# Loads of gate i and x per chunk of 1024 tokens in a gated linear recurrence with a causal gated unit

## The chip, the cores and the metric

The kernel runs on one core of a Trainium2 chip. The metric is the device time of one execution in microseconds (us), taken as the median of several runs. The core has a matrix engine (PE, whose weight loads are listed as PEld), a vector engine (DVE), an activation engine (ACT), a general engine (POOL), a queue that issues transfers (SP) and 16 DMA engines that all transfers share.

## What is computed

The inputs have 4 sequences of 6336 tokens with 256 channels, in fp32. A linear recurrence over time runs first, and its result `y` goes through a gated unit with a causal convolution of five taps:

```python
log_a = 8.0 * sigmoid(r_gate) * np.log(np.clip(sigmoid(a_param), 1e-06, 1.0 - 1e-06))
a_t = np.exp(log_a)
norm = np.sqrt(np.maximum(1.0 - a_t * a_t, 1e-06))
x_gated = norm * sigmoid(i_gate) * x
for t in range(S):
    h = a_t[:, t] * h + x_gated[:, t]
    y[:, t] = h
# then, with x = y:
for k in range(5):
    gate_pre += conv_w[k] * xp[:, k:k + S, :]      # xp is x with four zero tokens ahead
out = (1.0 / (1.0 + np.exp(-gate_pre)) * (x @ w_val)) @ w_out
```

Three inputs (r, i, x) are read and one output is written, 25.95 MB each.

## The kernel before

**Tiling.** The 25344 tokens of all sequences are laid end to end and cut into 28 chunks: 256, 256 and 512 tokens, 23 chunks of 1024, and again 512 and 256. A chunk of 1024 is two windows of 512; there are 51 windows. Recurrence, roots and norm go by chunk, and the gated unit and its output go by window.

**Layouts.** A load puts tokens on the partitions: partition p holds consecutive tokens of its stretch, each with 256 channels. The recurrence needs channels on the partitions and time along the row, so work goes back and forth through transposes on PE, which write to PSUM (8 banks of 2 KB a partition).

**Rings.** `rring`, `iring` and `xring` have four slots each, a slot being one window (512 tokens, 4 KB a partition). The r load already takes a whole chunk in one transfer of 1 MB: partition p gets eight consecutive tokens, 8 KB, spread over two neighbouring slots (`of_chunk`, L281). The loads of i and x go window by window (`load`, L276): 512 KB, four consecutive tokens or 4 KB for each partition.

**Steps of a chunk or window**, by their names in the order:

- `lr`, `li`, `lx`: loads by SP. `ta` (L297) and `tb` (L300): tanh of r and i on ACT, for a whole chunk.
- `tr` (L345): PE transposes the tanh of r; `ex` (L359): ACT makes the decay `a` of it, in fp32, in the order of time, into `aring`.
- `sq` (L367): POOL squares the decay into `ering`; `rt` (L392): ACT takes the square root for a batch of up to four chunks and writes the norm as bf16. This needs another table of functions on ACT, so a table load (L543) stands before and after.
- `nt` (L406): PE transposes the norm back to tokens on partitions. The bf16 norm is taken as words of 4 B, each holding two neighbouring tokens of one channel, so a window of 512 tokens has 256 words and one transpose takes 128 of them: word q of every partition, that is every second word of the window's row.
- `pp`, `up` (L307, L319): POOL adds 1 to the tanh of i and multiplies by x, into `uring`. For six windows at the start and later (0 to 3, 8, 10) PE (`xp`, L324) copies x to PSUM and DVE (`uv`, L333) does the work.
- `xg` (L417): DVE multiplies the norm, out of PSUM, into `uring`, for a chunk. The last three chunks go another way (L421), without `nt`.
- `xt` (`words`, L431): PE transposes the words of `uring` to time along the row, each transpose writing every second word of its window in PSUM. `sc` (L464): DVE runs the recurrence as a scan over the chunk, once for each half of the channels.
- `cv` (L476): PE does the convolution, `tg` (L483): ACT the gate's tanh; `vl` (L491): PE the value product; `gv` (L496): DVE gate times value; `ou` (L506): PE the output product; `cd` or `ca` (L514, L516): DVE or ACT copies it out of PSUM; `st` (L527): SP stores it.

**Order.** `ORDER` is a list written out by hand or program beforehand; it is walked once, and each word emits the instructions of one step (the number after `@` are PSUM banks). Every engine runs its own instructions in that order, waiting where a buffer or an input isn't ready. SP's queue holds loads and stores together in the order, so one that waits for a slot holds up those behind it. The table of ACT functions is switched where the list asks for another.

Of the kernel before, what the change touches and what calls it, by code (L numbers as in the profile page):

```python
# [8 lines left out]
P = 128  # L9
CONV_K = 5  # L10
FP32 = mybir.dt.float32
# [13 lines left out]
NU = 10  # L25
NRI = 4
# [15 lines left out]
s_ident s_small s_kt s_diag lr.0 lr.2 lr.1 li.0 li.1 ta.0 ta.2 lr.3 tr.0.0@1 ex.0.0 ta.1 tr.2.0@1 tb.0 tr.2.1@4 lr.5  # L42
tr.1.0@2 li.2 ex.2.1 tr.1.1@6 tr.0.1@7 lx.2 ex.0.1 lx.0 ex.1.1 sq.0.1 ex.1.0 sq.1.1 ex.2.0 sq.2.1 ta.3 sq.0.0 sq.1.0
tb.1 lr.7 ta.4 li.4 li.3 lx.3 s_wl.3 tb.2 tr.3.0@6,7 s_wl.0 lx.1 ex.3.0 lr.9 tr.3.1@4,5 xp.0@2 ex.3.1 sq.3.0 li.6 uv.0
ta.5 s_wl.2 sq.2.0 sq.3.1 xp.2@2,3 lx.4 uv.2 tb.3 li.5 sq.4.1 s_wl.1 xp.3@6,7 uv.3 xp.1@1 sq.4.0 rt.0.0 lx.5 uv.1 li.7
li.8 pp.4 rt.1.0 nt.0@7 nt.2@6 xg.0 lx.6 nt.1@1 xt.0.1@4 xt.0.0@7 xg.1 xg.2 xt.1.1@2 sc.0.0 xt.2.1@5 up.4 xt.1.0@1
sc.1.0 sc.0.1 nt.3@6,7 sc.1.1 s_wcast lx.8 ta.6 lr.11 sc.2.1 cv.0@2,3 xt.2.0@4 cv.1@0,1 sc.2.0 tb.4 lr.13 xg.3 vl.1@4,5
tg.1 li.10 pp.5 tg.0 xt.3.1@6 gv.1 lx.7 tb.5 xt.3.0@7 pp.6 sc.3.1 tr.5.0@2,3 up.6 ex.5.0 tr.5.1@4,5 li.11 li.12
vl.0@0,1 gv.0 pp.7 sc.3.0 lx.10 ex.5.1 li.9 nt.4@0,1 up.5 ou.0.0@3 ou.1.0@2 ta.7 cd.0.0 cv.3@4,5 cd.1.0 st.0 sq.6.0
xg.4 lx.9 cv.2@6,7 tg.3 lr.15 tg.2 sq.5.1 st.1 vl.2@0,1 xt.4.0@3 ta.8 gv.2 cv.4@4,5 sq.5.0 sc.4.0 tg.4 lr.17 tr.7.0@6,7  # L50
xt.4.1@1 ex.7.0 sq.6.1 tr.7.1@4,5 sc.4.1 ex.7.1 xp.8@2,3 up.7 lx.12 uv.8 ou.2.0@6,7 cv.5@0,1 tb.6 sq.7.1 cd.2.0
vl.5@4,5 tb.7 li.13 sq.8.0 vl.4@2,3 lx.11 li.14 gv.4 tg.5 xp.10@6,7 li.16 sq.8.1 uv.10 st.2 li.15 ou.4.0@2,3 lx.14 gv.5
sq.7.0 rt.2.0 vl.3@6,7 gv.3 ou.5.0@0,1 pp.9 cd.4.0 pp.11 cd.5.0 rt.2.1 ou.3.0@2,3 up.9 cd.3.0 st.5 nt.5@6,7 xg.5
nt.6@0,1 up.11 lx.13 cv.6@2,3 st.3 xg.6 xt.5.0@5 xt.5.1@0 pp.12 lx.15 sc.5.0 tg.6 up.12 tb.8 xt.6.1@2 sc.5.1 nt.7@4,5
ta.10 pp.14 up.14 xg.7 ta.9 cv.8@6,7 lr.21 sc.6.1 xt.7.1@5 pp.13 tg.8 lr.19 vl.6@0,1 lx.16 tb.9 up.13 li.17 gv.6
tr.9.0@6,7 li.18 lx.18 sc.7.1 ex.9.0 li.19 pp.15 tr.9.1@0,1 lx.17 xt.6.0@4 li.20 pp.16 cv.7@2,3 ex.9.1 sc.6.0 sq.9.0
xt.7.0@5 st.4 ou.6.0@6,7 tg.7 up.15 vl.8@0,1 sc.7.0 ta.12 cv.9@2,3 sq.9.1 tg.9 cd.6.0 vl.7@4,5 ta.11 gv.7 nt.8@2,3
sq.10.0 xg.8 vl.9@6,7 tb.10 lr.23 st.6 tr.11.0@4,5 up.16 gv.9 lr.25 tr.11.1@2,3 ex.11.0 gv.8 ou.9.0@6,7 pp.18 cd.9.0
ou.7.0@0,1 ex.11.1 pp.17 xt.8.0@5 cd.7.0 sq.11.0 ou.8.0@6,7 st.7 xt.8.1@0 cd.8.0 tb.11 li.22 cv.11@2,3 lx.19 sq.10.1
sc.8.1 st.8 cv.10@6,7 tg.11 lx.20 li.21 ta.13 cv.12@2,3 li.23 sq.12.0 sc.8.0 tg.12 vl.12@0,1 lr.27 up.17 tg.10 li.24  # L60
vl.11@2,3 gv.11 vl.10@4,5 sq.11.1 rt.3.0 gv.10 sq.12.1 gv.12 ou.10.0@4,5 cd.10.0 ou.11.0@2,3 up.18 rt.3.1 cd.11.0
ou.12.0@4,5 cd.12.0 pp.19 lx.22 nt.9@0,1 st.10 xg.9 pp.20 lx.21 nt.10@6,7 st.11 up.19 xg.10 st.9 xt.9.1@5 xt.9.0@2
sc.9.1 cv.13@6,7 ta.14 up.20 tg.13 sc.9.0 lr.29 nt.11@4,5 tb.12 cv.14@6,7 xg.11 tg.14 li.26 pp.22 tr.13.1@2,3 st.12
xt.10.1@0 tb.13 li.25 up.22 sc.10.1 vl.14@4,5 lx.23 cv.15@6,7 ex.13.1 li.28 lx.24 pp.21 gv.14 vl.13@0,1 pp.24 tg.15
gv.13 vl.15@4,5 sq.14.1 ta.15 xt.10.0@7 gv.15 tr.13.0@0,1 sc.10.0 cv.16@2,3 sq.13.1 ex.13.0 lr.31 li.27 ou.13.0@4,5
up.21 ta.16 cd.13.0 ou.14.0@6,7 ou.15.0@0,1 cd.14.0 tg.16 lr.33 sq.13.0 nt.12@4,5 lx.25 cd.15.0 tb.14 xt.11.0@7 st.13
lx.26 xg.12 tr.15.0@2,3 pp.23 st.14 ex.15.0 tr.15.1@0,1 sc.11.0 up.23 cv.18@4,5 tg.18 xt.11.1@2 pp.25 sc.11.1 ex.15.1
vl.18@6,7 cv.17@4,5 up.24 tg.17 gv.18 vl.17@2,3 sq.14.0 lx.28 tb.15 li.29 gv.17 vl.16@0,1 st.15 xt.12.1@5 gv.16 pp.26
ta.17 li.31 ou.17.0@6,7 lx.27 cv.20@2,3 sc.12.1 sq.15.1 li.30 ta.18 cv.19@0,1 sq.16.0 cd.17.0 tg.20 ou.16.0@4,5 cd.16.0
tg.19 sq.15.0 vl.19@6,7 xt.12.0@2 gv.19 st.16 lr.37 vl.20@0,1 sq.16.1 lr.35 sc.12.0 rt.4.0 li.32 ou.18.0@6,7  # L70
ou.19.0@4,5 up.26 gv.20 cd.19.0 rt.4.1 up.25 nt.13@2,3 cd.18.0 nt.14@0,1 xg.13 pp.27 lx.29 cv.21@4,5 lx.30 xg.14 pp.28
st.19 xt.13.1@7 st.17 sc.13.1 up.27 st.18 tr.17.0@2,3 tg.21 ou.20.0@0,1 tb.16 up.28 lx.31 cd.20.0 vl.21@6,7 xt.13.0@4
ex.17.0 gv.21 li.34 tr.17.1@0,1 li.33 pp.29 sc.13.0 lx.32 nt.15@6,7 pp.30 ex.17.1 ou.21.0@2,3 sq.17.0 xt.14.0@5 xg.15
xt.14.1@4 ta.19 cv.22@0,1 sc.14.1 up.29 tg.22 lr.39 vl.22@6,7 tb.17 cv.23@0,1 sq.17.1 gv.22 sc.14.0 cv.24@6,7 tg.23
li.35 pp.32 lx.33 tg.24 li.36 pp.31 vl.23@0,1 ca.21.0 gv.23 up.30 ou.22.0@6,7 ta.20 xt.15.0@5 cd.22.0 cv.26@0,1 up.31
# [31 lines left out]
def kernel(  # L107
# [74 lines left out]
    with tc.manual_schedule():  # L182
# [101 lines left out]
        def op_li(w):  # L284
            load(w, "i")

        def op_lx(w):
            load(w, "x")
# [286 lines left out]
```

## Time and profile before

| what | value |
|---|---|
| median of three runs | 285.41 us (285.11 to 285.95) |
| the profiled execution's own time | 286.67 us |
| its span, from the first to the last instruction | 284.9 us |
| granted TensorE clock, mean | 1.000 |
| HBM read / written | 78.39 MB / 25.95 MB |
| packets of DMA queue q1 | 26640 |

The profile lists for each engine its busy time; for groups of instructions (by line, engine, operation and shape) the count, the busy time, the mean duration of one in ns, and how long the engine sat idle before them and on whom it waited. A timeline row gives start, length and count of a run of like instructions. A window row gives the busy time of each engine, with the number of instructions, in a stretch of the span. Matmuls are pipelined: a matmul's duration is longer than the pace at which they follow one another.

### The profile page before, as it was taken

What the parts mean: (1) busy time and instruction counts of PE and PEld (TensorE: products, weight loads), DVE (VectorE), ACT (ScalarE), POOL (GpSimd) and SP (SyncE); (2) the same over time, 40 slices, a digit from 0 to 9 for tenths busy, and PEclk for the clock granted to TensorE, in tenths of its full rate; (3) what the DMA queues carried; (4) which work ended last, traced back from release to release, by engine and by line L of the source; (5) the groups of instructions that cost most, each with busy time, mean ns of one, the idle gap of its engine ahead of it and who ended that gap; (6) DMA issues with size and microseconds to landing.
All of it is one profiled execution on the core that took longest, in us unless ns stands there. A gap on an engine that the chain in (4) does not pass through costs nothing.

```text
span 284.9 us, 6194 instructions
## 1 busy us (share of the span) xinstructions
PE 241.9 (85%) x2493; PEld 164.8 (58%) x2493; DVE 245.5 (86%) x203; ACT 270.9 (95%) x192; POOL 234.3 (82%) x156
## 2 busy tenths in 40 slices
PE   1268778978789878998979998899899899999993
PEld 1243565656548456684557585656665655956562
DVE  2005997899999899999999999999999999999980
ACT  7899999999999999999999999999999999999673
POOL 1429689999999996999999999998999978993200
PEclk9999999999999999999999999999999999999999
DMA  7899999999999999999999999989999999914466
GB/s 235 329 414 382 379 419 404 420 409 415 370 407 384 416 426 414 418 423 412 419 427 411 418 414 415 420 313 358 410 416 422 412 384 345 350 81 147 187 240 242
DMA packets 26682, 104.74 MB, mean 368 GB/s; under 512 B 2967, under 2 KB 3486, under 8 KB 23710
## 3 DMA queue, kind: packets, MB, share of 16 engines
q1 hardware_dynamic: 26640, 104.35, 92.6%
q8 instruction: 19, 0.31, 0.4%
q14 instruction: 9, 0.07, 0.1%
q10 hardware_dynamic: 14, 0.01, 0.0%
HBM read 78.39 MB, written 25.95 MB: 366 GB/s over the span
## 4 chain that ended last, share of the span: by engine, by line
ACT 37%; PE 17%; DMA 16%; issue 15%; DVE 13%; ACTq 0%; DVEq 0%
DMA iring<-in_i_gate_dram 10%; ACT taring L297 8%; ACT tgring L483 8%; DVE yring L464 7%; ACT tbring L300 6%; ACT aring L359 6%; DMA rring<-in_r_gate_dram 6%; ACT ering L392 5%; PE banks L506 5%; PE banks L476 4%; PE banks L491 3%; ACT L543 2%; DVE uring L417 2%; PE banks L406 2%; DVE tgring L496 2%
## 5 line engine op out<-in xcount | busy, mean ns | idle before, releaser
L367 POOL TENSOR_TENSOR ering<-aring 128x1024 f32<-128x1024 f32 (+2 forms) x55 | 91.9, 1696 | 14.8 <-ACT aring L359 14.8
L464 DVE TENSOR_TENSOR_SCAN yring<-aring,yring,banks 128x1024 bf16<-128x1024 f32 (+5 forms) x48 | 98.2, 2059 | 1.4 <-PE banks L431 0.9
L319 POOL TENSOR_TENSOR uring<-tbring,xring 128x1024 bf16<-128x1024 bf16 (+1 forms) x45 | 95.7, 2140 | 4.2 <-DMA xring<-in_x_dram 3.3
L496 DVE SCALAR_TENSOR_TENSOR tgring<-tgring,banks 128x1024 bf16<-128x1024 bf16 (+1 forms) x51 | 59.1, 1181 | 7.8 <-PE banks L491 4.8
L476 PE MATMUL banks<-yring,diag 64*64 64x512 bf16 (+7 forms) x1080 | 62.1, 361 | 3.5 <-DVE yring L464 1.2
L307 POOL TENSOR_SCALAR tbring<-tbring 128x1024 bf16<-128x1024 bf16 (+1 forms) x45 | 46.3, 1041 | 15.1 <-ACT tbring L300 14.9
L506 PE MATMUL banks<-wo,tgring 128*128 128x256 bf16 x396 | 50.6, 273 | 6.2 <-DVE tgring L496 3.5
L491 PE MATMUL banks<-yring,wv 128*128 128x512 bf16 (+4 forms) x216 | 49.5, 361 | 5.2 <-DVE yring L464 1.9
L359 ACT ACTIVATE aring<-banks,khf 128x2048 f32<-128x2048 bf16 (+3 forms) x34 | 52.8, 1611 | 0.3 <-PE banks L345 0.2
L483 ACT ACTIVATE tgring<-banks 128x1024 bf16<-128x1024 f32 (+1 forms) x51 | 50.1, 1004 | 2.2 <-PE banks L476 2.0
L506 PEld LDWEIGHTS <-tgring 128*128 128x128 bf16 x396 | 41.9, 114 | 15.8 <-issue 8.0
L297 ACT ACTIVATE taring<-rring 128x2048 bf16<-128x2048 f32 (+2 forms) x28 | 47.8, 1719 | 1.8 <-DMA rring<-in_r_gate_dram 1.8
L300 ACT ACTIVATE tbring<-iring 128x2048 bf16<-128x2048 f32 (+2 forms) x28 | 48.0, 1719 | 0.5 <-DMA iring<-in_i_gate_dram 0.5
L476 PEld LDWEIGHTS <-diag 64*64 64x64 bf16 x1080 | 29.3, 106 | 27.0 <-issue 10.2
L392 ACT ACTIVATE ering<-ering 128x4096 bf16<-128x4096 f32 (+2 forms) x14 | 44.5, 3220 | 0.1
L514 DVE COPY oring<-banks 128x1024 f32<-128x1024 f32 (+1 forms) x33 | 38.2, 1179 | 1.3 <-DMA out_dram<-oring 1.1
L345 PE MATMUL banks<-ident_b,taring 128*128 128x128 bf16 x396 | 28.7, 230 | 11.0 <-ACT taring L297 8.8
L491 PEld LDWEIGHTS <-wv 128*128 128x128 bf16 x216 | 19.6, 97 | 27.5 <-issue 13.2
L345 PEld LDWEIGHTS <-taring 128*128 128x128 bf16 x396 | 25.8, 103 | 14.7 <-ACT taring L297 10.7
L431 PE MATMUL banks<-ident,uring 128*128 128x128 f32 x198 | 30.3, 279 | 3.9 <-DVE uring L417 1.7
L406 PE MATMUL banks<-ident,ering 128*128 128x128 f32 x184 | 26.5, 289 | 5.3 <-ACT ering L392 3.2
L417 DVE TENSOR_TENSOR uring<-banks,uring 128x2048 bf16<-128x2048 bf16 (+2 forms) x25 | 27.8, 1127 | 1.4 <-PE banks L406 1.1
(39 smaller groups left out, 137.8 us busy)
## 6 DMA issues: line engine op xcount, KB each, us to landing
iring<-in_i_gate_dram SPq DMA_DIRECT2D x48, 512.0 KB, 10.0
xring<-in_x_dram SPq DMA_DIRECT2D x48, 512.0 KB, 9.5
out_dram<-oring SPq DMA_DIRECT2D x48, 512.0 KB, 8.9
rring<-in_r_gate_dram SPq DMA_DIRECT2D x23, 1024.0 KB, 8.9
rring<-in_r_gate_dram SPq DMA_DIRECT2D x2, 512.0 KB, 7.0
rring<-in_r_gate_dram SPq DMA_DIRECT2D x3, 256.0 KB, 3.7
iring<-in_i_gate_dram SPq DMA_DIRECT2D x3, 256.0 KB, 5.1
xring<-in_x_dram SPq DMA_DIRECT2D x3, 256.0 KB, 4.4
```

Of the source, the lines that this page charges most:

```text
L297: nc.scalar.activation(**tangent(c, taring, NTR, rring, NRI))
L300: nc.scalar.activation(**tangent(c, tbring, NTI, iring, NII))
L319: nc.gpsimd.tensor_tensor(out=u, in0=t1, in1=xt, op=ALU.mult)
L359: nc.scalar.activation(out=dst, in_=src, func=ACT.Exp, scale=khf[:, h:h + 1], bias=khf[:, h:h + 1])
L367: nc.gpsimd.tensor_tensor(out=e, in0=a, in1=a, op=ALU.mult)
L392: nc.scalar.activation(out=ering[:].bitcast(BF16)[:, 4 * o:4 * o + 2 * n], in_=ering[:, 2 * o:2 * o + 2 * n], func=ACT.Sqrt, scale=-0.25, ...
L464: nc.vector.tensor_tensor_scan(out=yring[:, h, col:col + o1 - o0], data0=aring[:, h, a_at[c] + o0:a_at[c] + o1], data1=xT[:, o0:o1], initi ...
L476: nc.tensor.matmul(out=gp[oh * 64:oh * 64 + 64, h, a:b], lhsT=diag[half * 64:half * 64 + 64, h, k, :], rhs=yring[half * 64:half * 64 + 64, ...
L483: nc.scalar.activation(out=tgring[:, w % NTG, :, 0:wins[w]], in_=live.pop(("gp", w))[:, :, 0:wins[w]], func=ACT.Tanh, scale=0.5)
L491: nc.tensor.matmul(out=val[:, m, a:b], lhsT=wv[:, hk, m * P:(m + 1) * P], rhs=yring[:, hk, col:col + b - a], start=(hk == 0), stop=(hk == ...
L496: nc.vector.scalar_tensor_tensor(out=tgring[:, w % NTG, :, 0:wins[w]], in0=tgring[:, w % NTG, :, 0:wins[w]], scalar=1.0, in1=live.pop(("va ...
L506: nc.tensor.matmul(out=ops[:, j * D:(j + 1) * D], lhsT=gv[:, hk, j:wins[w]:J], rhs=wo[:, hk, :], start=(hk == 0), stop=(hk == H - 1))
```

## The change

The loads of i and x go by chunk as r's do: one transfer for a chunk, 1 MB with 8 KB for each partition where the chunk has 1024 tokens. So partition p now holds eight consecutive tokens of a chunk of 1024, in two slots of the ring, instead of four of each window. A window's slots hold half of the tokens of each partition, and the steps that go from tokens to time have to follow: in `nt` and in `words` the q-th word of a partition is now found with a step of the chunk's words per partition (four for a chunk of 1024) instead of the window's (two). `xring` is placed like the other rings.

```diff
-        def load(w, which):
-            n = wins[w]
-            J = n // P
-            dst = xring[:, w % NX, 0:J, :] if which == "x" else iring[:, place(w, NII), 0:J, :]
-            nc.sync.dma_start(dst, flat[which][wstart[w]:wstart[w] + n, :].rearrange("(p j) d -> p j d", p=P))
+        def load(w, which, ring, n):
+
+            c = chunk_of[w]
+            nc.sync.dma_start(of_chunk(ring, n, c),
+                              flat[which][cstart[c]:cstart[c] + clen[c], :].rearrange("(p j) d -> p j d", p=P))
...
         def op_li(w):
-            load(w, "i")
+            load(w, "i", iring, NII)
 
         def op_lx(w):
-            load(w, "x")
-
+            load(w, "x", xring, NX)
+
+        def pairs_of(c):
+
+            nq = wins[cwins[c][0]] // (2 * P)
+            return [(w, q, nq * k + q, nq * len(cwins[c])) for k, w in enumerate(cwins[c]) for q in range(nq)]
...
-            for w in cwins[c]:
-                nq = wins[w] // (2 * P)
-                o = live["n", c] + (wstart[w] - cstart[c]) // 2
-                for q in range(nq):
-                    for h in range(H):
-                        e = o + h * clen[c] // 2
-                        nc.tensor.transpose(out=bank[:, k:k + P], in_=ering[:, e + q:e + wins[w] // 2:nq], identity=ident[:])
-                        k += P
+            for _, _, q, step in pairs_of(c):
+                for h in range(H):
+                    e = live["n", c] + h * clen[c] // 2
+                    nc.tensor.transpose(out=bank[:, k:k + P], in_=ering[:, e + q:e + clen[c] // 2:step], identity=ident[:])
+                    k += P
...
-            for w in cwins[c]:
-                nq = wins[w] // (2 * P)
-                o = (wstart[w] - cstart[c]) // 2
-                for q in range(nq):
-                    nc.tensor.transpose(
-                        out=out[:, o + q:o + wins[w] // 2:nq],
-                        in_=uring[:, (w + 1) % NU, q, h * P:(h + 1) * P, :].rearrange("p d two -> p (d two)")
-                        .bitcast(FP32),
-                        identity=ident[:])
+            for w, q, at, step in pairs_of(c):
+                nc.tensor.transpose(out=out[:, at:clen[c] // 2:step],
+                                    in_=uring[:, (w + 1) % NU, q, h * P:(h + 1) * P, :]
+                                    .rearrange("p d two -> p (d two)").bitcast(FP32),
+                                    identity=ident[:])
```

The order is written anew. Besides the loads (28 of i and 28 of x instead of 51 each), windows 0 and 3 are multiplied on POOL (`pp`, `up`) instead of through PE and DVE (`xp`, `uv`); the root of the last batch is taken in two places (`rt.7.0` for chunk 25, `rt.7.1` later for 26 and 27) with table loads around each; and steps stand earlier or later by some places throughout. The batches and the number of the other steps stay as they are. The stretch of the order from the second batch's roots, before and after:

```diff
-sq.7.0 rt.2.0 vl.3@6,7 gv.3 ou.5.0@0,1 pp.9 cd.4.0 pp.11 cd.5.0 rt.2.1 ou.3.0@2,3 up.9 cd.3.0 st.5 nt.5@6,7 xg.5
-nt.6@0,1 up.11 lx.13 cv.6@2,3 st.3 xg.6 xt.5.0@5 xt.5.1@0 pp.12 lx.15 sc.5.0 tg.6 up.12 tb.8 xt.6.1@2 sc.5.1 nt.7@4,5
+gv.3 vl.5@6,7 sq.8.1 gv.5 xp.10@4,5 rt.2.0 uv.10 sq.7.1 ou.5.0@0,1 cd.5.0 ou.4.0@4,5 pp.11 cd.4.0 ou.3.0@2,3 up.9
+rt.2.1 cd.3.0 nt.5@4,5 xg.5 nt.6@6,7 pp.12 lx.13 st.4 xg.6 xt.5.1@2 st.5 up.12 sc.5.1 nt.7@6,7 tb.8 xt.5.0@0 up.11
```

More of the change, by code (lines that the diff above doesn't have):

```diff
@@ L47 @@
[L47 to L51, printed above, removed]
```

119 lines of the change are left out of this document (60 added, 59 removed).

## The prediction

> **What bounds the kernel now.** I read the totals by engine first, then the stages, then the waits.
>
> ```profile
> span 284.9 us, 6194 instructions
> PE 241.9 (85%) x2493; PEld 164.8 (58%) x2493; DVE 245.5 (86%) x203; ACT 270.9 (95%) x192; POOL 234.3 (82%) x156
> ...
> core 0: us, PE busy (x) PEld busy (x) DVE busy (x) ACT busy (x) POOL busy (x), PEclk, DMA share, GB/s
> 60.00:220.00 160.00, 142.36 (x1537) 99.37 (x1536) 156.29 (x118) 159.30 (x99) 155.96 (x96) 1.00 1.01 406
> 220.00:260.00 40.00, 38.08 (x405) 25.99 (x407) 39.18 (x30) 39.87 (x35) 36.02 (x24) 1.00 0.75 289
> 260.00:285.00 25.00, 19.98 (x210) 12.76 (x202) 17.17 (x17) 15.74 (x17) 1.80 (x2) 0.99 0.60 232
> ```
>
> Averages hide three stages. From 60 to 220 us ACT is busy 159.30 of 160 us, so it bounds; DVE (idle 3.7 us) and POOL (idle 4.0) stand right behind it, the DMA engines are occupied throughout, and PE has 17.6 us of room. From 220 to 260 ACT and DVE are full and PE has only 1.9 us left. From 260 on ACT has 9 us of idle time and the end comes over PE, DVE and ACT in turn.
>
> ```profile
> ACT 37%; PE 17%; DMA 16%; issue 15%; DVE 13%; ACTq 0%; DVEq 0%
> ...
> ACT tgring L483 <- PE banks L476: 2.0, 3, 1.4
> ACT taring L297 <- DMA rring<-in_r_gate_dram: 1.8, 3, 0.8
> ACT tbring L300 <- DMA iring<-in_i_gate_dram: 0.5, 1, 0.5
> POOL uring L319 <- DMA xring<-in_x_dram: 3.3, 2, 2.7
> DVE uring L417 <- PE banks L406: 1.1, 3, 0.5
> SPq L276 <- POOL uring L319: 33.0, 14, 5.7
> ```
>
> First the shares of the chain of waits, then the waits (total us, times, longest). The engines hardly wait for loads: 2.3 us on ACT, 3.3 on POOL, out of 285. The chain gives DMA 16%, but those loads land just in time; little is lost to them. So what loads gain is worth at most these few us, and what delays DVE or ACT in the middle counts almost at once.
>
> **The change part by part.** *Fewer, larger loads.* Loads of i and x fall from 102 to 56 issues, and of a chunk of 1024 tokens each partition gets one piece of 8 KB where it got two of 4 KB. Two stretches of 5 us, the first (100 to 105) with 4 KB pieces alone, the second (145 to 150) with mostly 8 KB pieces of the r load:
>
> ```profile
> DMA packets 577, 2.10 MB, mean 419 GB/s; under 512 B 65, under 2 KB 65, under 8 KB 577
> DMA packets 369, 2.17 MB, mean 434 GB/s; under 512 B 39, under 2 KB 39, under 8 KB 171
> ```
>
> That is 3.6% more rate. On the 48 MB of the loads that become large (2 x 23 x 1024 KB) it saves 48.2/0.419 - 48.2/0.434, about 4 us of DMA time. ACT waited only 2.3 us for loads, 1.8 of it for r, whose loads stay as they are. I take 0; bounds 0 to -2.3 us. The input gate's tanh always took both halves in one instruction, so one landing in place of two costs it nothing.
>
> *x as one transfer.* Its two slots must both be free now, so SP holds the load until the second window's multiplication (L319) has run, and everything behind it in SP's queue (r, i and stores) waits too. The release comes later by one `pp` and one `up`:
>
> ```profile
> L319 POOL TENSOR_TENSOR uring<-tbring,xring 128x1024 bf16<-128x1024 bf16 x44 | 94.5, 2161 | 4.1 <-DMA xring<-in_x_dram 3.3
> L307 POOL TENSOR_SCALAR tbring<-tbring 128x1024 bf16<-128x1024 bf16 x44 | 45.7, 1051 | 6.8 <-ACT tbring L300 6.7
> xring<-in_x_dram SPq DMA_DIRECT2D x48, 512.0 KB, 9.5
> L543 ACT ACT_TABLE_LOAD x14 | 18.0, 1283 | 0.2
> ```
>
> That is 3.2 us later, and the first half lands 1.25 us later (512 KB at 419 GB/s). A chunk takes about 11 us (284.9 over 25 chunks' worth), the slots hold two, and POOL waited for x twice in the whole run. I take 0, covered by those slots; if the cover is gone, up to 4.5 us a chunk (rival below).
>
> *Windows 0 and 3 from DVE and PE to POOL.* POOL gets 3.2 us for window 3 and about half for window 0; DVE and PE lose three blocks. POOL sat idle 7.1 us just before its long squares and 2.7 after them:
>
> ```profile
> 19.73 8.45 POOL L367 TENSOR_TENSOR ering<-aring 128x1024 f32<-128x1024 f32 x5 [7.14 <-ACT aring L359]
> 31.88 2.15 POOL L319 TENSOR_TENSOR uring<-tbring,xring 128x1024 bf16<-128x1024 bf16 x1 [2.69 <-DMA xring<-in_x_dram]
> ```
>
> Cost 0, hidden there; if not, 3.2 us.
>
> *The order.* The roots of the last batch are taken in two goes, chunk 25 first: two more table loads, 2 x 1.283 = 2.6 us on ACT. In the order they stand near the end, where ACT idles 9 us; uncovered they cost 2.6. What the earlier root may bring is bounded by waiting it can remove: ACT's waits for the gate's convolution, 2.0 us in the run. I take -0.6; bounds -2.0 to +2.6. The other moves carry the same instructions; copies on ACT stay 18, the square there stays one.
>
> *The transposes.* This is where I see the cost. A word is two tokens in 4 B. Partition p now holds eight tokens of the chunk, so `nt` picks every fourth word out of `ering` (16 B apart) where it picked every second (8 B); `xt` writes to PSUM with the same step, reading contiguously.
>
> ```profile
> L406 PEld LDWEIGHTS banks<-ident,ering x184: 141/209/219, 28.5 to 245.4; 128*128 128x128 f32 x184
> L431 PEld LDWEIGHTS banks<-ident,uring x198: 137/140/153, 29.4 to 270.9; 128*128 128x128 f32 x198
> ...
> 146.12 1.99 PEld L406 LDWEIGHTS banks<-ident,ering 128*128 128x128 f32 x16 [1.90 <-ACT ering L392]
> ...
> 29.43 0.20 PEld L431 LDWEIGHTS banks<-ident,uring 128*128 128x128 f32 x2
> 37.15 0.86 PEld L431 LDWEIGHTS banks<-ident,uring 128*128 128x128 f32 x8 [0.80 <-DVE uring L417]
> ```
>
> Min, median, max in ns. The operand of `nt` is the one loaded as weights: 141 ns at its least, 209 as a rule, against 140 for the contiguous operand of `xt`. Pace: 16 loads in 1.99 us are (1990 - 209)/15 = 119 ns apart; two contiguous loads in 0.20 us are 60 ns apart. The step of two words doubled the load's pace. Eight `xt` take (860 - 140)/7 = 103 ns each although they write PSUM with a step of two, so I charge the output's step nothing (from below 0; from above at most as much as `nt`). For step four, bounds: 119 ns (nothing more is lost) and 240 ns (it doubles again, like 60 to 119). I take 240, since the trace's one comparison of steps showed a doubling.
>
> The Trainium skill, "SBUF — State Buffer", Door 1, says that SBUF is read in lines of 16 bytes, that two hits on a line are needed for full rate, and that "each access that crosses to a new line pays a penalty". Step two still makes two hits, and the trace shows 119 ns instead of 60, so the measurement is harsher than the rule; step four makes one, so by the rule too this change is where a penalty falls. No run so far shows step four.
>
> So each chunk of eight transposes takes 8 x 0.12 = 0.97 us more, 22 chunks 21 us of PE. From 60 to 220 PE's room takes its share; the latency is another matter, as DVE's multiplication (L417) takes what `nt` made:
>
> ```profile
> 64.17 2.08 PE L406 MATMUL banks<-ident,ering 128*128 128x128 f32 x16
> 65.51 2.35 DVE L417 TENSOR_TENSOR uring<-banks,uring 128x2048 bf16<-128x2048 bf16 x2
> ...
> 85.45 1.23 PE L406 MATMUL banks<-ident,ering 128*128 128x128 f32 x8 [0.42 <-ACT tgring L483]
> 86.81 1.23 DVE L417 TENSOR_TENSOR uring<-banks,uring 128x2048 bf16<-128x2048 bf16 x1 [0.46 <-PE banks L406]
> ...
> 105.79 2.08 PE L406 MATMUL banks<-ident,ering 128*128 128x128 f32 x16
> 107.13 2.35 DVE L417 TENSOR_TENSOR uring<-banks,uring 128x2048 bf16<-128x2048 bf16 x2
> ...
> 146.12 2.18 PE L406 MATMUL banks<-ident,ering 128*128 128x128 f32 x16 [1.64 <-ACT ering L392]
> 148.07 2.35 DVE L417 TENSOR_TENSOR uring<-banks,uring 128x2048 bf16<-128x2048 bf16 x2
> ...
> 225.28 2.32 PE L406 MATMUL banks<-ident,ering 128*128 128x128 f32 x16 [0.57 <-ACT ering L392]
> 226.61 2.36 DVE L417 TENSOR_TENSOR uring<-banks,uring 128x2048 bf16<-128x2048 bf16 x2 [0.36 <-PE banks L406]
> ...
> 236.16 0.74 PE L406 MATMUL banks<-ident,ering 128*128 128x128 f32 x4 [0.32 <-DVE yring L464]
> 237.14 1.22 DVE L417 TENSOR_TENSOR uring<-banks,uring 128x2048 bf16<-128x2048 bf16 x1
> ...
> 244.70 1.12 PE L406 MATMUL banks<-ident,ering 128*128 128x128 f32 x8
> 246.23 1.20 DVE L417 TENSOR_TENSOR uring<-banks,uring 128x2048 bf16<-128x2048 bf16 x1
> ```
>
> The pair of chunks begun at 64.17 ends at 66.25, with 1.93 added at 68.18; DVE's second multiplication began half way, at 66.7: 1.5 us late. Worked out in the same way the pairs at 105.8 and 146.1 are 1.5 and 1.0 late, the single chunk at 85.5 is 0.8 late and one more like it, at 168.6, as much: 5.6 us before 220. Behind the waiting multiplication stand DVE's scans, which feed the convolution, which feeds ACT's gate tanh. DVE's 3.7 us of idle time can absorb that much: 1.9 left. At 225.28 the pair ends at 229.5 against a start at 227.8, 1.8 late, the chunk at 245, with 0.97 added, is 0.6 late, and the one at 236, whose first four had 0.3 us to spare and keep 0.16 of their added 0.48, is 0.4 late: 2.8, less DVE's 0.8 of idle time in that stage, 2.0.
>
> Sum: 1.9 + 2.0 - 0.6 = +3.3 us. The profiled execution took 286.67 us with a span of 284.9 (1.8 lie around it); 286.67 + 3.3 = 290.0. It stands 1.26 over the median of the runs, 285.41; so 288.7.
>
> **The rivals.** *The step costs nothing more* (119 ns stays). For it: the PSUM step shows no cost at all. Against: the doubling above. Then only the gains are left, -0.6 to -4.3 with all of ACT's load waits gone; at half of those waits, 285.41 - 0.6 - 1.2 = 283.6, faster. It decides at a pace under about 150 ns: then 5.6 us shrinks to 1.4 and fits into DVE's idle time.
>
> *Nothing is absorbed.* Idle time of DVE lies elsewhere than the lateness, and ACT has none to give back: 5.6 + 2.8 - 0.6 = 7.8, so 293.2. For it: ACT, DVE and POOL are 97% busy or more from 60 to 220. Against: the order also moves transposes and multiplications apart.
>
> *x lands late.* The held load passes POOL's slack. For it: SP already waits 33 us for POOL's releases. Against: only two waits for x, early. From the point where POOL's 4.0 us of idle time are used, about 0.2 us a chunk, it costs in full; at 0.5 us for 22 chunks 11 - 4 = 7 us, 292.4.
>
> *The step costs, but the new order hides it*: the two cancel, 285.4.
>
> **How the numbers follow.** Forecast 43%; step free 30%, of which 5 no change; nothing absorbed 12%; x late 5%; cancelled 10%. A measurement of this kernel tells about 0.3% (0.86 us) from no change. Faster 25%, within 0.3% 15%, slower 60%. The range takes in the free step with most of its gains (283) and the unabsorbed case (294); the forecast's own range is 286.5 to 292.
>
> **What would show it.** Weight loads of the norm's transposes near 345 ns at the median and sixteen of them in nearly 4 us would show the step right; 209 ns and 2 us would prove it wrong, and with it the forecast. Then DVE must show idle time before the multiplication, released by PE, of some us more than 1, and ACT more than 2 us in waits for the convolution. ACT's busy time should be 273.5 with 16 table loads, the first i and x loads of 1024 KB should land in about 10 us, and POOL's wait for x stay under 5 us. Wrong otherwise: if ACT stays as full as now up to 260 us, the step's cost lay off its path.

## The result, and the profile after

| | before | after |
|---|---|---|
| median of 11 runs each | 285.43 us (284.38 to 288.05) | 288.77 us (287.19 to 295.67) |
| ratio, 95% interval | | 1.0101 (1.0066 to 1.0135) |
| the profiled execution's own time | 286.67 us | 287.96 us |
| its span | 284.9 us | 286.2 us |

The ratio leaves out the changed kernel's run of 295.67 us, which is more than 1.5% above its fastest; the ratios below leave out such runs too.

The changed kernel is about 1% slower. The predicted 288.7 us was met almost exactly, but the path to it was not: the term that made most of the sum did not occur, and the order of the steps, which the sum had costed at nothing, took its place.

First the totals by engine of the kernel after, and the stages (start and end of the stretch in us, its length, then PE, weight loads, DVE, ACT and POOL with busy time and instructions, granted clock, share of the DMA engines, GB/s):

```profile
span 286.2 us, 6058 instructions
PE 241.7 (84%) x2465; PEld 165.5 (58%) x2487; DVE 243.8 (85%) x200; ACT 273.4 (96%) x194; POOL 241.0 (84%) x160
```

```profile
30.00:60.00 30.00, 26.83 (x271) 18.48 (x274) 26.11 (x27) 29.04 (x20) 27.63 (x21) 0.94 0.96 386
60.00:220.00 160.00, 142.88 (x1527) 100.49 (x1539) 154.52 (x118) 158.84 (x98) 155.37 (x94) 1.00 1.00 403
220.00:260.00 40.00, 38.20 (x382) 26.01 (x387) 39.56 (x31) 39.52 (x34) 35.92 (x24) 1.00 0.87 329
260.00:288.00 28.00, 21.35 (x231) 13.09 (x229) 19.33 (x18) 19.63 (x21) 4.77 (x4) 0.97 0.45 178
```

In the kernel before ACT was busy 159.30 us of the second of these stages and 39.87 of the third (shown with the prediction); the row of its first was:

```profile
30.00:60.00 30.00, 25.62 (x276) 17.33 (x277) 25.91 (x27) 29.47 (x20) 26.74 (x18) 1.00 1.02 412
```

ACT's idle time from 30 to 260 us was 0.53 + 0.70 + 0.13 = 1.36 us before and is 0.96 + 1.16 + 0.48 = 2.60 us after. That is 1.24 us more, and the profiled execution is 1.29 us longer. ACT still bounds, and what it loses ahead of 260 us is what the run loses. After 260 us ACT is busy 3.9 us longer (19.63 against 15.74): 2.6 us is what the two more table loads add to its whole run, and 1.3 us is work that was done ahead of 260 us before. Its idle time there falls from 24.9 - 15.74 = 9.2 to 26.2 - 19.63 = 6.6 us, so the table loads lie in idle time, as the prediction had it.

Where ACT lost that time is seen in its timeline. These are all the gaps that it shows between 25 and 262 us, first before, then after (start, length, line and operation; in brackets the idle time just before, and what ended it):

```profile
38.41 1.91 ACT L300 ACTIVATE tbring<-iring 128x2048 bf16<-128x2048 f32 x1 [0.48 <-DMA iring<-in_i_gate_dram]
96.12 1.91 ACT L297 ACTIVATE taring<-rring 128x2048 bf16<-128x2048 f32 x1 [0.45 <-DMA rring<-in_r_gate_dram]
```

```profile
35.52 0.60 ACT L475 ACTIVATE tgring<-banks 128x512 bf16<-128x512 f32 x1 [0.39 <-PE banks L468]
49.26 1.91 ACT L296 ACTIVATE taring<-rring 128x2048 bf16<-128x2048 f32 x1 [0.48 <-DMA rring<-in_r_gate_dram]
86.97 1.91 ACT L296 ACTIVATE taring<-rring 128x2048 bf16<-128x2048 f32 x1 [0.94 <-DMA rring<-in_r_gate_dram]
249.27 1.01 ACT L508 COPY oring<-banks 128x1024 f32<-128x1024 f32 x1 [0.22 <-PE banks L498]
```

Two of the four new gaps, 1.42 of 2.03 us, are waits for r, whose loads keep their size and were only moved in the order. The first, 0.39 us behind PE, goes with a low clock of PE in this execution (last section). The waits by engine (total us, times, longest) say the same, and so do the issues (count, size, median us from issue to landing):

```profile
ACT taring L296 <- DMA rring<-in_r_gate_dram: 3.0, 4, 1.4
POOL uring L318 <- DMA xring<-in_x_dram: 6.1, 5, 2.2
DVE uring L413 <- PE banks L402: 2.2, 5, 0.9
ACT tgring L475 <- PE banks L468: 0.7, 2, 0.4
```

```profile
rring<-in_r_gate_dram SPq DMA_DIRECT2D x23, 1024.0 KB, 10.1
iring<-in_i_gate_dram SPq DMA_DIRECT2D x23, 1024.0 KB, 9.8
xring<-in_x_dram SPq DMA_DIRECT2D x23, 1024.0 KB, 9.8
```

The same row of the kernel before has r landing after 8.9 us:

```profile
rring<-in_r_gate_dram SPq DMA_DIRECT2D x23, 1024.0 KB, 8.9
```

How a load of unchanged size comes to land later is seen at the second wait. In the chain of waits of the kernel after stands the transfer that ended it (issue, us until landing), and SP's own timeline shows what had been issued just ahead of it:

```profile
74.91 11.98 DMA rring<-in_r_gate_dram
```

```profile
71.31 0.34 SPq L273 DMA_DIRECT2D iring<-in_i_gate_dram  x1
73.11 0.34 SPq L273 DMA_DIRECT2D rring<-in_r_gate_dram  x1
73.50 0.48 SPq L273 DMA_DIRECT2D xring<-in_x_dram  x1
74.91 0.33 SPq L273 DMA_DIRECT2D rring<-in_r_gate_dram  x1
```

Four loads of 1 MB go out within 3.6 us, and at the 403 GB/s of this stage each occupies the DMA engines for 2.6 us. The last of them is the r load that ACT could have used at 86.97 - 0.94 = 86.0 us; the i load at the head, 3.6 us ahead of it, was not used until 88.8. In the kernel before the two r loads went first:

```profile
73.39 2.13 SPq L281 DMA_DIRECT2D rring<-in_r_gate_dram  x2
75.60 0.38 SPq L276 DMA_DIRECT2D xring<-in_x_dram  x1
```

The term that was forecast is missing. The weight loads of `nt` (min, median, max in ns), and sixteen of them in a row:

```profile
L402 PEld LDWEIGHTS banks<-ident,ering x184: 180/211/230, 28.5 to 246.6; 128*128 128x128 f32 x184
```

```profile
65.03 2.01 PEld L402 LDWEIGHTS banks<-ident,ering 128*128 128x128 f32 x16 [1.03 <-ACT ering L391]
```

The median is 211 ns where 209 was measured before, and the pace is (2010 - 211)/15 = 120 ns where it was 119. The prediction named 345 ns as the sign that its step was right, and 209 ns as the sign that it was wrong.

### The profile page after: what moved, and what is told of

The parts are those of the page before. It is cut to its first block, busy times and chain, and to the rows that moved or that the text cites. A ratio compares the mean times of both kernels' runs of the same rounds, so it can differ in the third digit from the quotient of the medians.

```text
span 286.2 us, 6058 instructions
## 1 busy us (share of the span) xinstructions
PE 241.7 (84%) x2465; PEld 165.5 (58%) x2487; DVE 243.8 (85%) x200; ACT 273.4 (96%) x194; POOL 241.0 (84%) x160
## 4 chain that ended last, share of the span: by engine, by line
ACT 41%; PE 20%; issue 13%; DMA 11%; DVE 10%; POOL 4%; ACTq 0%; DVEq 0%
DMA rring<-in_r_gate_dram 11%; ACT tgring L475 8%; ACT tbring L299 7%; ACT aring L358 7%; ACT taring L296 7%; ACT ering L391 7%; PE banks L468 6%; PE banks L498 4%; PE banks L483 4%; DVE tgring L488 4%; POOL ering L366 3%; DVE yring L456 3%; ACT L535 3%; DVE oring L506 2%; PE banks L424 2%
## 5 line engine op out<-in xcount | busy, mean ns | idle before, releaser
L318 POOL TENSOR_TENSOR uring<-tbring,xring 128x1024 bf16<-128x1024 bf16 (+1 forms) x47 | 98.9, 2116 | 6.9 <-DMA xring<-in_x_dram 6.1
L468 PE MATMUL banks<-yring,diag 64*64 64x512 bf16 (+7 forms) x1080 | 63.1, 361 | 2.4 <-DVE yring L456 0.8
L306 POOL TENSOR_SCALAR tbring<-tbring 128x1024 bf16<-128x1024 bf16 (+1 forms) x47 | 49.7, 1067 | 12.2 <-ACT tbring L299 9.8
L498 PE MATMUL banks<-wo,tgring 128*128 128x256 bf16 x396 | 51.2, 274 | 3.7 <-DVE tgring L488 2.7
L483 PE MATMUL banks<-yring,wv 128*128 128x512 bf16 (+4 forms) x194 | 48.3, 359 | 5.8 <-ACT tgring L475 3.2
L475 ACT ACTIVATE tgring<-banks 128x1024 bf16<-128x1024 f32 (+1 forms) x51 | 50.8, 1012 | 0.9 <-PE banks L468 0.7
L468 PEld LDWEIGHTS <-diag 64*64 64x64 bf16 x1080 | 29.9, 106 | 26.6 <-issue 11.3
L344 PE MATMUL banks<-ident_b,taring 128*128 128x128 bf16 x396 | 30.1, 230 | 13.4 <-ACT taring L296 11.7
L402 PE MATMUL banks<-ident,ering 128*128 128x128 f32 x184 | 28.2, 302 | 3.6 <-DVE tgring L488 1.2
L402 PEld LDWEIGHTS banks<-ident,ering 128*128 128x128 f32 x184 | 25.1, 211 | 8.9 <-ACT ering L391 5.0
## 6 DMA issues: line engine op xcount, KB each, us to landing
rring<-in_r_gate_dram SPq DMA_DIRECT2D x23, 1024.0 KB, 10.1
```

The lines of the kernel that those rows point to most:

```text
L318: nc.gpsimd.tensor_tensor(out=u, in0=t1, in1=xt, op=ALU.mult)
L468: nc.tensor.matmul(out=gp[oh * 64:oh * 64 + 64, h, a:b], lhsT=diag[half * 64:half * 64 + 64, h, k, :], rhs=yring[half * 64:half * 64 + 64, ...
L475: nc.scalar.activation(out=tgring[:, w % NTG, :, 0:wins[w]], in_=live.pop(("gp", w))[:, :, 0:wins[w]], func=ACT.Tanh, scale=0.5)
L483: nc.tensor.matmul(out=val[:, m, a:b], lhsT=wv[:, hk, m * P:(m + 1) * P], rhs=yring[:, hk, col:col + b - a], start=(hk == 0), stop=(hk == ...
L498: nc.tensor.matmul(out=ops[:, j * D:(j + 1) * D], lhsT=gv[:, hk, j:wins[w]:J], rhs=wo[:, hk, :], start=(hk == 0), stop=(hk == H - 1))
```

## Experiments

Each kernel was timed in five rounds next to the kernel before on the same chip, and the ratios are to that kernel. Four questions were open: is it the loads or the order; does the step cost anything; which part of the order costs; and is it the landing of loads that ACT pays for.

**The order alone.** The kernel before, loads by windows, with the new order.

```diff
-s_ident s_small s_kt s_diag lr.0 lr.2 lr.1 li.0 li.1 ta.0 ta.2 lr.3 tr.0.0@1 ex.0.0 ta.1 tr.2.0@1 tb.0 tr.2.1@4 lr.5
...
+s_ident s_small s_kt s_diag lr.0 lr.2 lr.1 li.1 li.0 ta.0 ta.2 lr.3 tr.0.0@3 tr.0.1@7 ta.1 ex.0.1 lr.5 tr.1.1@2
+tr.2.0@0 ex.0.0 li.2 tr.1.0@1 ex.1.1 tr.2.1@3 lx.0 ex.2.0 ex.2.1 tb.1 ex.1.0 tb.0 ta.3 li.3 li.4 pp.0 sq.2.0 sq.1.0
...
```

> The kernel before with the changed order; each load of a chunk stands as two window loads of 512 KB one after the other at its place. If the new order costs (a later r load, two more table loads), it takes as long as the changed kernel: about 288 us, 2 to 3.5 us over before. If the large transfers cost, it stays within 1 us of before, 285.4. If the step of four words costs, likewise, since the step is two here.

Measured: 1.0091 (1.0057 to 1.0125). The order by itself costs what the whole change costs. The two r waits are there, and a longer one for i at 209 us:

```profile
48.94 1.91 ACT L298 ACTIVATE taring<-rring 128x2048 bf16<-128x2048 f32 x1 [0.49 <-DMA rring<-in_r_gate_dram]
86.35 1.91 ACT L298 ACTIVATE taring<-rring 128x2048 bf16<-128x2048 f32 x1 [0.63 <-DMA rring<-in_r_gate_dram]
209.20 1.91 ACT L301 ACTIVATE tbring<-iring 128x2048 bf16<-128x2048 f32 x1 [1.59 <-DMA iring<-in_i_gate_dram]
222.85 1.02 ACT L484 ACTIVATE tgring<-banks 128x1024 bf16<-128x1024 f32 x1 [0.88 <-PE banks L507]
```

The first two are those of the changed kernel, though no load is larger than before: it is the order that makes them. This profiled execution took 290.78 us against a median of 289.19, so the last two need not be in every run.

**The loads alone.** The changed kernel in the old order; a load of 1 MB stands where the later of its two window loads stood.

```diff
-sq.2.0 sq.3.1 xp.2@2,3 lx.4 uv.2 tb.3 li.5 sq.4.1
+sq.2.0 sq.3.1 xp.2@2,3 lx.3 uv.2 tb.3 li.5 sq.4.1
...
```

> The changed kernel with the order of before; each chunk's load of i or x stands where the second window's load stood. If large transfers cost by themselves (landing late, holding up SP's queue), 287 to 290 us, and ACT and POOL wait more than 5 us for DMA. If only the order costs, 285 to 286. If the 8 KB pieces gain with the order left alone, 283 to 285.

Measured: 1.0348 (1.0298 to 1.0398), more than any case of the prediction. Its waits, its stage from 30 to 60 us, and the load that its chain of waits shows there:

```profile
PE banks L324 <- DMA xring<-in_x_dram: 6.6, 1, 6.6
POOL uring L319 <- DMA xring<-in_x_dram: 6.3, 7, 2.4
ACT tgring L476 <- PE banks L469: 6.3, 4, 4.3
```

```profile
30.00:60.00 30.00, 25.04 (x244) 16.38 (x246) 23.66 (x25) 23.88 (x16) 21.30 (x15) 0.92 0.91 348
```

```profile
21.44 9.29 DMA xring<-in_x_dram
```

Window 3 goes by PE (`xp`), and its x now comes with that of window 4 in one load, which is issued only at 21.44 us, when both slots are free. PE waits 6.6 us for it. PE works in order, so all that stands behind comes late too, down to ACT's gate tanh of the first windows (a wait of 4.3 us), and ACT loses 29.47 - 23.88 = 5.6 us in this stage, most of the 9 us. So x does land late in the old order, as in the rival of that name, but it is PE that waits, at one place early in the run. In the new order, which multiplies windows 0 and 3 on POOL, ACT is busy 29.04 us in the same stage: the pair of the two edits costs 1.0%, one edit alone 3.5%, the other 0.9%.

**The same order with half transfers.** As the changed kernel, but i and x of a chunk of 1024 tokens come in two transfers of 4 KB pieces; layout and step stay.

```diff
+            src = flat[which][cstart[c]:cstart[c] + clen[c], :].rearrange("(p k j) d -> p k j d", p=P, k=2)
+            for k, v in enumerate(cwins[c]):
+                nc.sync.dma_start(ring[:, place(v, n), :, :], src[:, k])
```

> The changed kernel, order and step of four words kept, but every chunk of 1024 tokens loads i and x in two transfers of 512 KB with 4 KB pieces. If the size of a transfer costs, it comes back by 2 us or more against the changed kernel, to 286 or less. If the order or the step costs, it stays at 288 to 289.

Measured: 1.0164 (1.0125 to 1.0202). In this order and layout one transfer is no worse than two; it looks about 0.6% better, though the intervals overlap a little.

**The roots of the last batch together.** The changed kernel with two squares moved up and the second part of the root right behind the first, so 14 table loads.

```diff
-up.49 xt.25@4,5 rt.7.0 gv.41 vl.43@2,3 sq.26.0 gv.43
+up.49 sq.26.0 sq.27.1 xt.25@4,5 rt.7.0 rt.7.1 gv.41 vl.43@2,3 gv.43
...
-pp.50 ou.43.0@4,5 sq.27.1 tg.45
+pp.50 ou.43.0@4,5 tg.45
...
-gv.44 rt.7.1 ou.45.0@6,7
+gv.44 ou.45.0@6,7
```

> The changed kernel with the last batch's two roots one right behind the other (the squares of chunks 26 and 27 moved ahead of them), so two table loads of 1.28 us fewer on ACT. If those loads are on the path, 2 to 2.6 us less than the changed kernel, about 286. If the end is bound by PE, or chunk 25's earlier root pays for them, no less than 0.5 us gained, or even slower by up to 1 us.

Measured: 1.0219 (1.0155 to 1.0282), from three of its six runs. Two table loads fewer bring nothing; the kernel gets slower still. Why it loses another 1.2% was not followed up.

**The step alone.** The kernel before, with `nt` picking every fourth word instead of every second; the normalised gate so meets x of other tokens of its chunk.

```diff
-            for w in cwins[c]:
-                nq = wins[w] // (2 * P)
...
+            step = clen[c] // (2 * P)
+            for q in range(step):
...
+                    nc.tensor.transpose(out=bank[:, k:k + P], in_=ering[:, e + q:e + clen[c] // 2:step], identity=ident[:])
```

> The kernel before with one edit: the norm's transposes of a chunk of 1024 tokens pick every fourth word instead of every second (the normalised gate so meets x of other tokens of the same chunk; the work is the same). If the step of four costs as the prediction had it (240 ns a load where the step of two takes 119), sixteen loads take about 3.9 us, DVE's multiplication behind them comes later and the kernel is 3 to 8 us slower, ratio 1.011 to 1.027. If a step of four costs no more than one of two, the pace stays at 120 ns, the median of the loads at 209 to 211 ns and the ratio at 1.000, give or take 0.003.

Measured: 0.9985 (0.9962 to 1.0009).

```profile
L404 PEld LDWEIGHTS banks<-ident,ering x184: 139/210/226, 28.4 to 246.0; 128*128 128x128 f32 x184
```

A step of four words costs nothing over a step of two. This settles the step of the prediction that carried the sum.

**The order by parts.** The kernel before with the new order up to the second part of the third root (64 us) and the old one after it; and the other way, the new order only from the seventh root (227 us) on. At these two points both orders have emitted almost the same steps, so they can be joined.

```diff
-tr.2.0@1 tb.0 tr.2.1@4 lr.5 tr.1.0@2 li.2 ex.2.1 tr.1.1@6 tr.0.1@7 lx.2 ex.0.1 lx.0
+tr.2.0@0 ex.0.0 li.2 tr.1.0@1 ex.1.1 tr.2.1@3 lx.0 ex.2.0 ex.2.1 tb.1 ex.1.0 tb.0
...
```

> The kernel before, loads by windows of 512 KB, with the changed kernel's order up to the second part of the third batch's root (about 64 us) and the old order from there on. If the order's loss arises at the start (windows 0 and 3 on POOL, the r load of chunk 8 issued 3 us later, ACT up to 0.6 us late at that root), it is slower by 0.3 to 1.1 us, ratio 1.001 to 1.004. If the loss arises later (in the run of the whole new order ACT first fell behind by more than 0.5 us at 206 us, at a wait for i), the ratio is 1.000, give or take 0.003.

```diff
-xg.22 xt.21.1@1 pp.44 cv.38@4,5 sc.21.1 up.44 ou.36.0@2,3 xt.21.0@0 cv.37@6,7 sc.21.0
+xg.22 xt.21.0@3 xt.21.1@1 pp.44 sc.21.0 cv.38@6,7 up.43 xt.22.0@0 tg.38 sc.21.1
...
```

> The kernel before with the old order up to the second part of the seventh batch's root (about 227 us) and the changed kernel's order from there on: the last root in two goes, so 16 table loads and not 14. If these two loads of 1.283 us are covered by ACT's idle time after 260 us, as the prediction had it, the ratio is 0.998 (the earlier root brings 0.6 us) to 1.001. If they lie on the path of the end, it is 1.5 to 2.6 us slower, ratio 1.005 to 1.009. If the whole loss of the new order arises before 227 us, the ratio is 1.000, give or take 0.003.

Measured: 1.0023 (0.9999 to 1.0048) for the start and 1.0012 (0.9985 to 1.0039) for the end. The two table loads are in the second. Neither can be told from no change. Together they make some 0.35% of the order's 0.91%; the rest would lie between 64 and 227 us, though the intervals leave room.

**r earlier.** The changed kernel with three pairs of steps put back, so that the two r loads of the waits above go out earlier.

```diff
-sc.1.1 nt.3@6,7 tb.4 xg.2
+sc.1.1 nt.3@6,7 ta.6 tb.4 lr.13 xg.2
...
-ta.9 li.17 pp.13 pp.14 ta.10 xg.7 lr.19
+ta.10 li.17 lr.21 pp.13 pp.14 ta.9 xg.7
...
-sc.7.0 ta.11 sq.10.1
+sc.7.0 ta.12 sq.10.1
...
```

> The changed kernel with three places of its order put back: the r gate's tanh of chunk 6 ahead of the input gate's of chunk 4 (so the r load of chunk 8 is issued about 2.7 us earlier), chunk 10 ahead of chunk 9 with the r load of chunk 12 first, and chunk 12 ahead of chunk 11, as before. If the late r loads are what the change costs, ACT's waits for r (0.48 us at 49.3, 0.94 at 87.0) and its wait for the gate's convolution at 35.5 go, the fourth root starts about 1 us earlier and the run is 1.0 to 1.4 us faster than the changed kernel, ratio 1.004 to 1.007 to the kernel before. If the waits only move to another load (i, x or a later r), the ratio stays at 1.008 to 1.012.

Measured: 1.0204 (1.0164 to 1.0243), outside what either theory expected: the kernel became 1% slower still. To move these two loads forward is no cure. The edit also changes the order in which ACT takes the chunks, and what moved with the loads may cost more than the two waits. The profile is of one of its longest executions, 295.97 us, and so can't price this; in it ACT still waits 1.11 us for r at 88 us, and 1.74 us for i at 48 us in place of 0.48 for r.

**A held load moved back.** In the changed kernel the i load of chunk 9 stood at the head of SP's queue until 55.86 us, for its slot, while an r load whose slots had been free since 44.0 us waited behind it, and the transfers fell to 309 GB/s between 50 and 57 us. Here only that queue is changed.

```diff
-sq.6.1 lr.17 tr.7.0@0,1
+sq.6.1 lr.15 lr.17 tr.7.0@0,1
...
-tg.4 li.15 sq.5.1 lx.11 tg.5 gv.4 tr.7.1@4,5 li.13 lr.15
+tg.4 sq.5.1 lx.11 tg.5 gv.4 tr.7.1@4,5 li.13 li.15
```

> The changed kernel with two loads moved in SP's queue and nothing else: the i load of chunk 9, which was held for the tanh of chunk 7 until 55.86 us, stands behind the x, i and r loads that had been free to go since 48.3, 48.8 and 44.0 us, and that r load ahead of the r load of chunk 10. If what the order costs is a hole in the transfers, made by a held load at the head of the queue, the share of the DMA engines from 30 to 60 us rises from 0.96 to 1.00 or more, the stretch from 50 to 57 us from 309 to about 400 GB/s, ACT's wait of 0.94 us for r at 87 us goes, and the run is 0.9 to 1.3 us faster than the changed kernel, ratio 1.005 to 1.007 to the kernel before. If the loss lies in the order of the engines' own work, the ratio stays at 1.008 to 1.012.

Measured: 1.0129 (1.0084 to 1.0173). The edit did what it should, and it did not help. The GB/s in 40 slices of the span (the eighth begins at 51 us), and three of ACT's gaps:

```profile
GB/s 240 345 418 396 406 416 362 420 421 276 423 420 426 420 419 315 420 424 404 414 422 414 327 419 421 425 421 412 337 410 196 364 432 413 196 340 126 87 278 254
```

```profile
87.20 1.91 ACT L297 ACTIVATE taring<-rring 128x2048 bf16<-128x2048 f32 x1 [0.83 <-DMA rring<-in_r_gate_dram]
...
208.21 1.91 ACT L297 ACTIVATE taring<-rring 128x2048 bf16<-128x2048 f32 x1 [0.88 <-DMA rring<-in_r_gate_dram]
210.97 1.91 ACT L300 ACTIVATE tbring<-iring 128x2048 bf16<-128x2048 f32 x1 [0.85 <-DMA iring<-in_i_gate_dram]
```

The hole in the eighth slice is filled (420) and another opens two slices on (276; 373 in the changed kernel). The wait at 49 us isn't there, the one at 87 us stays, and two open at 208 and 211 us. Filling this hole did not make the kernel faster, so it wasn't what the order costs.

**All loads in the order of their release**, in the changed kernel and in the kernel with the large loads and the old order. The cut is of the first; the second is edited in the same way.

```diff
-ex.13.0 ou.15.0@0,1 li.27 pp.24 xt.10.0@5 cd.15.0 pp.23
+li.27 lx.25 gv.15 ou.13.0@2,3 cd.13.0 st.13 ex.13.0 ou.15.0@0,1 pp.24 xt.10.0@5 cd.15.0 st.15 pp.23
...
-cd.14.0 sq.14.0 sc.10.0 xt.11.0@6 xt.11.1@7 tg.16 lr.33
+cd.14.0 st.14 lr.33 sq.14.0 sc.10.0 xt.11.0@6 xt.11.1@7 tg.16
...
```

> The changed kernel with all loads and stores that come free after 30 us issued in the order in which their slots came free in its profile; the engines' own order is untouched. If holes in the transfers are the cost, more bytes move by 220 us (86.6 MB in the changed kernel, 87.4 in the one before), ACT's waits for r and POOL's for x shrink and the ratio is 1.002 to 1.006. If it matters more that the load needed next goes first (stores and early loads now stand ahead of it), some wait for a load grows and the ratio is 1.010 or more.

> The kernel with the large loads and the old order (ratio 1.035), with the loads and stores that come free after 30 us issued in the order of their release. There the r load of chunk 7, free at 23.9 us, stood behind an x load held until 35.7, and the transfers ran at 285 GB/s from 28 to 36 us. If the held queue is what large loads cost in the old order, 3 to 6 us of its 9 come back, ratio 1.013 to 1.025. If the later releases themselves (both slots must be free) make the loss, the holes stay and the ratio is 1.030 to 1.040.

Measured: 1.0165 (1.0139 to 1.0191) and 1.0413 (1.0369 to 1.0458). The held queue explains neither. In the new order, first free, first served is worse than the written order. In the old one it brings nothing back; 1.0413 lies above the 1.030 to 1.040 that was expected for that case, though the intervals with and without the edit overlap (1.0348, to 1.0398). ACT's longest gap in the first of the two, the transfer that ended it as the chain of waits has it, and what SP had issued ahead of that:

```profile
139.88 1.91 ACT L297 ACTIVATE taring<-rring 128x2048 bf16<-128x2048 f32 x1 [2.35 <-DMA rring<-in_r_gate_dram]
```

```profile
127.31 12.48 DMA rring<-in_r_gate_dram
```

```profile
123.31 0.33 SPq L274 DMA_DIRECT2D iring<-in_i_gate_dram  x1
123.74 0.37 SPq L274 DMA_DIRECT2D xring<-in_x_dram  x1
124.30 2.77 SPq L520 DMA_DIRECT2D out_dram<-oring  x3
```

The r load is held by nothing, but an i load, an x load and three stores have gone out in the 4 us ahead of it, and it lands 12.48 us after its issue. This is the second wait of the changed kernel over again, in another place. ACT also waits 1.35 us for a store at 281 us there.

**Fewer bytes.** The changed kernel without the x loads of ten chunks, every second one from 6 to 24; these are computed from the x that stands in the slots.

```diff
+            if chunk_of[w] >= 6 and chunk_of[w] % 2 == 0 and len(cwins[chunk_of[w]]) == 2:
+                return
```

> The changed kernel with its order untouched, but the x loads of ten chunks of 1024 tokens (6, 8, 10 to 24) are left out, so these chunks are computed from the x that stands in the slots; 10 MB of 105 are not moved, and every instruction of the five engines stays. If what the change costs is loads that land late behind the other transfers, ACT's waits of 0.48 and 0.94 us for r at 49 and 87 us go, the seventh root starts at 221.5 us or earlier and the ratio to the kernel before is 0.999 to 1.004. If the loss lies in the order of the engines' own work or in the two table loads, the ratio stays at 1.007 to 1.012 though r lands early.

Measured: 1.0015 (0.9997 to 1.0033). With every engine's instructions in place and 10 MB fewer to move, the ratio falls from 1.0101 to 1.0015, and the two intervals lie apart. The engines' own work in the new order, step and table loads included, can thus be done in nearly the old time; that it is not points to the transfers. The other half of the expectation failed, as the timeline shows:

```profile
48.61 1.91 ACT L298 ACTIVATE taring<-rring 128x2048 bf16<-128x2048 f32 x1 [0.47 <-DMA rring<-in_r_gate_dram]
86.30 1.91 ACT L298 ACTIVATE taring<-rring 128x2048 bf16<-128x2048 f32 x1 [0.93 <-DMA rring<-in_r_gate_dram]
```

```profile
rring<-in_r_gate_dram SPq DMA_DIRECT2D x23, 1024.0 KB, 8.7
```

Both waits are still there, and the seventh root starts at 221.78 us, not by 221.5 (222.50 in the changed kernel, 221.60 before). The burst ahead of the second consists of the loads of chunks 10, 11, 9 and 12, and none of them was left out. But r lands in 8.7 us at the median again, not in 10.1. This profiled execution took 287.49 us, the longest of the kernel's twelve runs (285.62 to 287.49), so most of what the other runs won is not in its trace.

What stays open: which loads are late in the runs that were not profiled. The profile of the changed kernel explains 1.3 us, its median is 3.3 us above that of the kernel before. The waits at 206 to 211 us that the runs of the order alone (1.59 us), of the half transfers (1.28 and 0.82 us) and of the moved i load (0.88 and 0.85 us) show are a likely place, but that they occur in the changed kernel's other runs is argued, not shown. Nor was the kernel before run with fewer bytes. ACT's waits for loads there are 2.3 us in all, so if all of them went too, 0.8% of difference between the two orders could remain, and the last experiment would prove less than it seems to. Without the ten x loads SP's queue also has no waits for their slots, which this run does not tell from the bytes.

## Why the prediction was right, and where it was not

*What bounds the kernel*: right. ACT stayed the bound, and its lost time up to 260 us, 1.24 us, makes the profiled difference. The reading that "the engines hardly wait for loads", and that large loads could thus cost nothing, was the weak point: with the DMA engines occupied throughout, waits were few because the order fitted the landings, not because there was room: with the new order alone they grew.

*Fewer, larger loads* (0, bounds 0 to -2.3): the bound had the wrong side open. The queue's packet time, with packets, MB and share of 16 engines' span, before and after:

```profile
q1 hardware_dynamic: 26640, 104.35, 92.6%
```

```profile
q1 hardware_dynamic: 20016, 104.34, 92.0%
```

That is 0.926 x 284.9 = 263.8 us before and 0.920 x 286.2 = 263.3 us after: 0.5 us of transfer time less, not the 4 us worked out from 3.6% more rate. Even the 0.5 can't be put down to the pieces, as the order alone, all with the old pieces, has 0.911 x 288.9 = 263.2 us. The two stretches of 5 us compared there differed also in their small packets, 65 against 39 under 512 B. And r's landing, 1.2 us later at the median, was not thought of. It takes both edits: r lands in 9.2 us with the order alone, 9.3 with half transfers and 9.5 with the loads alone. Yet none of these three kernels is clearly faster than the changed one, so the median landing is not what sets the time.

*x as one transfer* (0, 4.5 us a chunk if the cover is gone): POOL waited 6.1 us instead of 3.3, above the 5 us that were set. In the new order none of ACT's gaps up to 262 us ends on POOL. In the old one x was late for PE instead, and that reached ACT, with 5.6 us lost from 30 to 60 us alone.

*Windows 0 and 3* (0) and *the order's start*: 0.23% (-0.01 to 0.48), so 0 to 1.4 us; right within what can be told.

*The root in two goes* (table loads covered, -0.6): covered, as forecast; ACT's busy time of 273.4 us was forecast as 273.5, and the new order's end measures 1.0012. ACT's waits for the convolution fell as was hoped, from 2.0 to 0.7 us, and to 0.5 with the order's end alone. But no gain of 0.6 us shows in the time: that kernel lies between 0.4 us faster and 1.1 slower.

*The other moves* ("carry the same instructions"): this is where the cost was. The count of instructions was right, but each moved load meets other transfers, which the sum put at nothing. The order alone measures 1.0091 with all transfers and the changed kernel 1.0015 with a tenth of them left out.

*The transposes* (240 ns taken, +1.9 and +2.0 us): wrong. This is the step that failed. A pace of 120 ns and a median of 211 ns were measured in the changed kernel, 119 and 210 in the kernel with the step alone. One doubling, from a step of one word to a step of two, was drawn on to a step of four. With it falls the lateness of DVE: it waited 2.2 us for `nt`, 1.1 more than before, not 5.6. The Trainium skill's "SBUF — State Buffer", Door 1, was weighed there as a reason for a penalty at step four; for this load by PE the runs show none beyond step two, so the measurement decides against that reading.

*The sum*, +3.3 us, thus matched +3.3 us of median by luck: a term of 3.9 us was not there, and the 0.9%, or 2.6 us, that the order costs was not in the sum. The rival "the step costs nothing more" had its condition met, a pace under 150 ns, and its time, 283.6, missed, because it too had the large loads and the new order as pure gain.

## What to carry to other kernels

Where one engine and the DMA engines are both full, price a moved or enlarged load by what it puts ahead of the others: each MB takes 2.6 us at 403 GB/s, and the r load that went out as the fourth of four within 3.6 us took 12 us to land, 0.9 too many. Few waits for loads in a profile can mean that order and landings fit, and need not mean that there is slack. A penalty seen between two values of a parameter should not be drawn on to a third; time that operand by itself first.

## What the runs showed of the hardware

8 KB pieces moved no faster than 4 KB pieces in sum: 263.3 us of all 16 DMA engines with 48 of the 104.3 MB changed to 8 KB, 263.8 and 263.2 us in two kernels without.

The granted TensorE clock in the first stage differed between executions with the same instructions. From 20 to 30 us, the changed kernel and the kernel with fewer x loads:

```profile
20.00:30.00 10.00, 5.99 (x10) 2.18 (x10) 2.53 (x4) 9.97 (x6) 10.00 (x6) 0.66 1.04 391
```

```profile
20.00:30.00 10.00, 5.76 (x13) 2.24 (x14) 2.97 (x6) 9.97 (x6) 10.00 (x7) 1.00 1.04 379
```

PE is busy 6 of 10 us in both, with a clock of 0.66 in one and 1.00 in the other. ACT was busy 9.97 us in both. From 28 to 32 us, again the changed kernel first:

```profile
28.00:32.00 4.00, 2.62 (x11) 2.23 (x12) 2.19 (x5) 3.98 (x3) 3.92 (x4) 0.50 1.04 371
28.00:32.00 4.00, 2.14 (x15) 1.72 (x16) 2.47 (x6) 3.98 (x3) 3.92 (x3) 1.00 1.03 349
```

Behind this stretch ACT waits 0.39 us for PE in the changed kernel, at 35.5 us, and not in the other. The kernel with the moved i load (0.50, a gap of 0.39 us) and the order alone (1.00, no gap) agree. So a third of what ACT loses up to 260 us in the profiled execution goes with the clock. It doesn't make the 3.3 us of the medians: a run of the changed kernel with a mean clock of 1.000 took 288.33 us. What sets the clock is open.
